# Routing in groups of four chunks, loads moved to SyncE, and transfers cut to 8 or 10 DMA engines, in a kernel of linear attention and experts on one core

## The chip, the cores and the metric

The kernel runs on one core of one Trainium2 chip. The metric is the device time of one execution in microseconds; lower is better. All times below are device microseconds.

## The reference

The first half is a linear attention with a 40 x 40 state per head, for 4 batches, 8 heads and 768 steps. The second half sends each of the resulting 3072 rows of 320 numbers to at most one of 8 experts.

```python
for t in range(S):                       # attention, S = 768, D = 40
    y[:, :, t] = np.einsum('bhd,bhde->bhe', rt, state)
    Sa = np.einsum('bhde,bhe->bhd', state, at)
    state_decay = state * wt[:, :, None, :] - np.einsum('bhd,bhe->bhde', Sa, bt)
    state = state_decay + np.einsum('bhd,bhe->bhde', vt, kt)
...
do_compute = x @ w_skip > 0              # experts, x is [3072, 320]
logits = xc @ w_gate; e_idx = np.argmax(logits, axis=1)
gate_w = probs[np.arange(len(xc)), e_idx]
h = np.maximum(xc[mask] @ w1[e], 0.0)    # w1 [8, 320, 1024], w2 [8, 1024, 320]
y[mask] = gate_w[mask, None] * (h @ w2[e])
out[do_compute] = xc + y
```

## The kernel before

**Attention.** The 768 steps are cut into 24 chunks of 32 steps. Two chunks are a pair h (12 of them), which is what `w`, `a`, `k`, `b` and `r` are loaded by. The loop `for c in range(NC)` in `attn` emits, for each chunk, a recurrence through the state: `ux` and `uq` (small matmuls, then ScalarE copies into the tile `R1t`, then a multiplication with a mask by GpSimd), `sst` (the new state), `rs`, and `yy`, which writes the 128 finished rows of the chunk into a tile `XS` and stores them from SyncE. Around it work for later chunks is spread: VectorE inverts the triangular factors (`tinv`, tiles `px` and `M`) and scans the decays, TensorE transposes and multiplies (`kbt`, `m1`, `m2`), GpSimd scales `k`, `b` and `a`.

**Routing.** `Moe.route` (from line 902 on) takes finished chunks: `xpose` transposes a chunk, `score` multiplies it with the 9 columns of skip and gate weights, `pick` finds the expert, and the rest ranks the rows within their expert, by a product of the one-hot rows `oh` with the triangle `s.tri` and with ones `s.one`. It adds a running `base` and scatters each chunk to a table `xg` by an indirect DMA from GpSimd. Before, one routing serves two chunks: eleven of them (started at c = 2, 4, ..., 22) and two of a single chunk at the end. Each `score` issues 12 matmuls per chunk, with 32 output rows each; the ranks take 8 matmuls per routing.

**Loads.** SyncE issues nearly all transfers, in the order of its queue. The function `load_rv` (line 357) loads `v` in the layout for the products with `r`, into `vvt`, `rrt` or `SCR`; `load_rr` (line 362) loads `r` into `rrt`; both take the issuing engine as an argument, which is GpSimd (`E=G`) from chunk 1 on. `cutl` loads rows 0 to 39 and 64 to 103 in two DMAs of 40 rows. `load_v` loads `v` a second time, as 16 pieces of 160 bytes in each of 32 rows, into `R1t`. `l1z` loads zeros, `idl` are constant blocks, `pad` fills the table `xg`, `load` (line 944) brings an expert's weights: of experts 0 and 1 at c = 20 and 22, of the others in the last part.

**The order.** Everything from the start up to chunk 21 is recorded by `Rec` and put in order by a planner (`Rec.plan`), a list schedule with costs of each instruction: `cost`, the transfer time of a DMA (`pipe`), a queue of DMA (`dq`), and a limit on how fast TensorE may go through blocks of 256 instructions, which take at least `BLK` us each (the constant `SLOW` stands beside it and is not used):

```python
pos+=t.k
while pos>=256*(blk+1):
    x=max(fin[i],ent+s.BLK); fin[i]=x; ent=x; blk+=1
```

The planner also may put a ScalarE copy out of PSUM on VectorE. Its order fixes the order on TensorE, ScalarE, VectorE, GpSimd and SyncE. A profile gives all recorded instructions the line of the call at the planner's end, L272, and those issued directly from chunk 22 on L134, which is the line of the recorder's call.

**Experts.** From about 490 us on the 8 experts are computed one after the other, in three products of rounded and remainder parts; the rows of each are scattered to the output by GpSimd.

Of the kernel before, what the change touches and what calls it, by code (L numbers as in the profile page):

```python
# [8 lines left out]
F32 = mybir.dt.float32  # L9
# [53 lines left out]
class Rec:  # L63
# [36 lines left out]
    def cost(s,e,op,w,r,a):  # L100
        sz=lambda x: int(np.prod([d[1] for d in list(x.ap)[1:]])) if len(list(x.ap))>1 else 1
        n=max(sz(x) for x in (w[:1]+r[:1]))
        if 'dma' in op: return (1.06,2.6) if 'ind' in op else (0.63 if e=='S' else 0.55,2.2)
# [12 lines left out]
        if op=='tensor_tensor_scan': return 0.02+0.00217*n,0  # L116
        if op=='transpose': return 0.08+0.00115*n*(1 if n<1000 else 1.6),0
        if op=='memset': return 0.04+0.0003*n,0
        if op=='reciprocal': return 0.17,0
        if op=='tensor_tensor': return (0.1 if ps and 'PSUM' not in str(w[0].space).upper() and n>199 else 0.06)+0.00105*n*(1 if ps or n<99 else 1.75),0  # L120
        return 0.12+0.00105*n,0
    def pipe(s,w,r):

        n=int(np.prod([d[1] for d in w.ap])); run=n
        for x in (w,r):
            q=1
            for st,k in reversed(list(x.ap)[0 if 'DRAM' in str(x.space).upper() else 1:]):
                if k>1 and st!=q: break
                q*=k
            run=min(run,q)  # L130
        p=w if 'DRAM' not in str(w.space).upper() else r
        return 4*n/min(6e5,5e3*max(16,p.ap[0][1]))+n/run*s.DSC/16
    def call(s,e,op,fn,a,k):
# [50 lines left out]
    def plan(s,keep=None):  # L184
# [33 lines left out]
        while done<N:  # L218
# [37 lines left out]
        s.st,s.fin,s.bank_of,s.en,s.span=st,fin,bank,en,max(fin)  # L256
    LET=0.7; FAR=1.0; ALT=1.0; FILL=None
    def keys(s):
# [46 lines left out]
def attn(ctx,tc,i,m,out,X):  # L305
# [50 lines left out]
    rvt={}  # L356
    def load_rv(c,E=G):
        if c>=NC: return
        t=VV[0] if c%2==0 else RR[1] if c==1 else VV[1]
        rvt[c]=t.rearrange("p (u t) -> p u t",u=16); cutl(E,rvt[c],i['vv'][c],c<4,128)  # L360
    rrt={}
    def load_rr(h,E=G):

        if h>=NH: return
        rrt[h]=RR[h%2].rearrange("p (u t) -> p u t",u=16); cutl(E,rrt[h],i['rr'][h],h<2,128)
    def load_v(c,x):
        if c>=NC: return
        SP.dma_start(R1[x][c%NR1][ao[x]:ao[x]+32,:,0:40],i['vt'][c,x])
    def scan_z(h,dst=None,E=None,rv=rv):
# [35 lines left out]
    def l1z(h,x):  # L405
        if h>=NH: return
        SP.dma_start(L1[x][h%NL][ao[x]:ao[x]+32].rearrange('p u c t -> p (u c t)'),i['zer'][0:32,0:1024])
    def l1a(h,x,E=None):
# [189 lines left out]
    def yy(c,x):  # L598
        if c<0: return
        if x==0: Yt[c]=ps_y.tile([128,8,40],F32,tag="py",name="psY")  # L600
        Y=Yt[c]
        R=R1[x][c%NR1]; l2=L2[x][(c//2)%NL2]; cc=c%2
        for hh in range(4):
            for b in range(4):
                u=4*b+hh
                TE.matmul(Y[32*b:32*b+32,2*hh+x,:],R[:,u,RW[cc]-32:RW[cc]],l2[:,cc,u,:],start=True,stop=True)
        if x==1:
            if cc==0: XS[c//2]=m.xp.tile([128,2,XW],F32,tag="XS",name="XS")
            xs=XS[c//2][:,cc,0:320]
            V.tensor_tensor(xs.rearrange("p (h e) -> p h e",h=8),Y,H[c//2]['WT',cc].rearrange("p h x e -> p (h x) e"),ALU.mult)  # L610
            SP.dma_start(ov[c],xs)
# [7 lines left out]
    if 1:  # L619

        with tc.manual_schedule(engines={ET.Pool}):
# [17 lines left out]
            for x in range(2): load_v(0,x)  # L639
            load_rv(0,SP); load_rr(0,SP); load_kb(2)  # L640
            scan_z(0,None,V); scan_d(0); scan_w(0,V); load_w(2)
# [8 lines left out]
            for x in range(2): l1a(1,x,V)  # L650
            load_a(2,L1t[:,3072:4096].rearrange("p (u t) -> p u t",u=16)); load_rv(1,SP)
            for b in range(4): kbt(0,b)
# [6 lines left out]
            for x in range(2):  # L659
                for c in range(2): SP.dma_start(L2[x][0][64*x:64*x+64,c],i['idl'][x,64*x:64*x+64])  # L660
            load_kb(3); load_w(3,alt[:,0:1041]); load_a(3,a1)
# [28 lines left out]
            for x in range(2):  # L690
                for c in range(2): SP.dma_start(L2[x][1][64*x:64*x+64,c],i['idl'][x,64*x:64*x+64])
        tg=iter(()); tn=[0]
# [154 lines left out]
class Moe:  # L847
# [46 lines left out]
    def route(s,XS,n,c0,last=None):  # L894
# [11 lines left out]
        yield  # L906
        rk=s.ps.tile([128,2*n,8],F32,tag="pp",name="rk")
# [233 lines left out]
```

## Time and profile before

| what | us |
|---|---|
| median of 3 runs | 624.01 (620.74 to 625.52) |
| the profiled execution | 625.9 |
| its span, first to last instruction | 624.0 |
| TensorE busy / VectorE busy | 470.0 / 472.7 |
| ScalarE busy / GpSimd busy | 390.0 / 315.5 |

The busy times are unions over the span. An engine can be idle in one stage and full in another, so the rows below are by stage. PE is TensorE's matmuls, PEld its weight loads, DVE VectorE, ACT ScalarE, POOL GpSimd, SPq SyncE's queue. `issue` is time in which an engine waited for nothing that the profile shows. A tile's name stands without its buffer number; the PSUM tiles are `pc`, `pq`, `ps`, `py`, `px`.

### The profile page before, as it was taken

Reading aid. Unit: us, or ns where it says so; the run is one execution under the profiler, and the core shown is the slowest. Engines: PE = TensorE matmul, PEld = TensorE weight load, DVE = VectorE, ACT = ScalarE, POOL = GpSimd, SP = SyncE. Lnnn points to the kernel's source line nnn. Section 1 sums busy time; section 2 is a strip of 40 time slices with the busy share of each in tenths; the row PEclk is TensorE's granted clock in tenths of the full one; section 3 lists DMA queues with packets and bytes.
Section 4 is the critical chain, followed back from the end, with each engine's and each line's share of the span. In section 5 each row is a group of like instructions: output and inputs, shape, how many; then the busy total and the mean of one; then the engine's idle time right before and its main releaser. Section 6 shows DMA issues by size and latency. Waiting matters only on the chain. (4 is left out here: it accounts for less than half of the span.)

```text
span 624.0 us, 28751 instructions
## 1 busy us (share of the span) xinstructions
PE 470.0 (75%) x12424; PEld 407.5 (65%) x12424; DVE 472.7 (76%) x1269; ACT 390.0 (62%) x982; POOL 315.5 (51%) x285
## 2 busy tenths in 40 slices
PE   0154327877787887887887789878977999999992
PEld 0143216666666666776776677667765799999992
DVE  6525894789997987998989879865783558898860
ACT  7073216878695877887696769577865455555510
POOL 4133626437491868477583853234223266666751
PEclk9997757899897998998798989989988999999997
DMA  8997232433452453425351534453663477775100
GB/s 190 251 270 226 78 99 65 130 81 92 93 137 75 108 143 100 133 67 147 87 153 40 144 98 109 101 153 95 167 168 93 123 220 232 240 225 156 43 18 18
DMA packets 64360, 80.59 MB, mean 129 GB/s; under 512 B 33698, under 2 KB 52719, under 8 KB 63124
## 3 DMA queue, kind: packets, MB, share of 16 engines
q1 hardware_dynamic: 58323, 64.55, 38.6%
q0 software_dynamic: 5904, 14.15, 8.2%
q8 instruction: 99, 1.62, 1.2%
q14 instruction: 34, 0.27, 0.1%
HBM read 67.80 MB, written 13.15 MB: 130 GB/s over the span
## 5 line engine op out<-in xcount | busy, mean ns | idle before, releaser
L272 ACT COPY R1t<-pc 32x288 f32<-32x288 f32 (+4 forms) x254 | 98.8, 389 | 38.1 <-PE pc L272 32.4
L272 POOL TENSOR_TENSOR R1t<-R1t,mc 64x512 f32<-64x512 f32 x43 | 55.5, 1292 | 70.9 <-ACT R1t L272 64.7
L272 DVE TENSOR_TENSOR px<-px,M 128x168 f32<-128x168 f32 (+10 forms) x240 | 61.2, 265 | 2.3
L134 POOL TENSOR_TENSOR WL<-WR,WH 128x1280 fp32r<-128x1280 f32 (+1 forms) x21 | 57.8, 2794 | 8.6 <-ACT WH L134 8.6
L272 POOL TENSOR_TENSOR WR<-WR,M 104x1024 f32<-104x1024 f32 x19 | 41.6, 2207 | 35.5 <-DVE M L272 22.9
L272 DVE TENSOR_TENSOR M<-M,px 128x168 f32<-128x168 f32 (+10 forms) x240 | 54.4, 255 | 2.0 <-DVE px L272 0.2
L272 DVE TENSOR_TENSOR_SCAN M<-M 104x1041 f32<-104x1041 f32 (+1 forms) x20 | 47.0, 2348 | 0.2
L272 ACT COPY R1t<-pq 32x256 f32<-32x256 f32 (+4 forms) x101 | 36.2, 358 | 8.4 <-PE pq L272 5.3
L134 ACT CAST WH<-WR 128x1024 fp32r<-128x1024 f32 (+1 forms) x35 | 39.6, 1132 | 0.0
L272 POOL DMA_INDIRECT xg<-XS,ix x20 | 24.1, 1206 | 29.9 <-DMA xg<-XS,ix 11.7
L134 POOL DMA_INDIRECT out<-ro,ti x16 | 15.8, 989 | 44.3 <-DVE ro L134 10.7
L272 PE MATMUL pc<-UX,TB 32*32 32x104 f32 (+1 forms) x1024 | 30.2, 245 | 9.0 <-issue 7.9
L134 ACT ACTIVATE hH<-pc 128x512 fp32r<-128x512 f32 x21 | 12.6, 599 | 37.8 <-PE pc L134 37.8
L134 DVE CAST ti<-xe 128x2 int32<-128x2 f32 x8 | 35.0, 4376 | 0.2
L272 PE MATMUL py<-L2t,R1t 128*32 128x40 f32 x1344 | 23.4, 208 | 12.1 <-issue 9.4
L134 PE MATMUL pc<-xH,WH 128*128 128x256 f32 x126 | 32.5, 283 | 0.0
L272 DVE TENSOR_TENSOR R1t<-pc,D 40x512 f32<-40x512 f32 (+1 forms) x44 | 26.6, 605 | 6.3 <-PE pc L272 4.2
L134 DVE TENSOR_TENSOR WL<-WR,WH 128x1024 fp32r<-128x1024 f32 (+1 forms) x19 | 23.8, 1253 | 9.9 <-ACT WH L134 9.4
L272 ACT COPY R1t<-ps 40x288 f32<-40x288 f32 (+4 forms) x72 | 27.5, 383 | 5.4 <-PE ps L272 4.2
L272 PE MATMUL ps<-R1t,L2t 128*40 128x72 f32 (+1 forms) x672 | 28.6, 233 | 2.8 <-ACT R1t L272 1.6
L272 PEld LDWEIGHTS pc<-UX,TB 32*32 32x32 f32 x1024 | 21.5, 107 | 14.0 <-issue 10.1
L272 PEld LDWEIGHTS py<-L2t,R1t 128*32 128x32 f32 x1344 | 17.7, 114 | 16.3 <-issue 11.7
(353 smaller groups left out, 1537.0 us busy)
## 6 DMA issues: line engine op xcount, KB each, us to landing
WR<-w SPq DMA_DIRECT2D x16, 640.0 KB
WR<-w SPq DMA_DIRECT2D x16, 512.0 KB
WR<-kb SPq DMA_DIRECT2D x16, 320.0 KB
WR<-w SPq DMA_DIRECT2D x16, 256.0 KB
R1t<-vt SPq DMA_DIRECT2D x48, 80.0 KB
out<-XS SPq DMA_DIRECT2D x24, 160.0 KB
rrt<-rr POOLq DMA_DIRECT2D x20, 160.0 KB, 5.4
vvt<-vv POOLq DMA_DIRECT2D x20, 160.0 KB, 6.1
```

The costliest lines, as they stand in the source:

```text
L134: if not s.on: return fn(*a,**k)
L272: for fn,a,k,own in s.tasks[i].calls: (fn if s.en[i]==s.tasks[i].e else s.nc.vector.tensor_copy)(*[at(x,own) for x in a],**{n:at(x,own) fo ...
```

## The change

1. One routing serves four chunks: `XS` holds four, routings start at c = 4, 8, 12, 16 and 20, one of two chunks at c = 22, and two of one chunk at the end as before. Twice as many steps of a routing are emitted per point.
2. `score` uses one matmul per third of the 320 columns with all 128 rows as output (3 per chunk, before 12). The ranks of a routing of n chunks take 1 + n matmuls with 128 output rows, which add up in PSUM what the running base of each further chunk was; VectorE adds the base once for all chunks and once for the next base. One memset is new.
3. `load_rv` and `load_rr` are issued from SyncE for every chunk.
4. The DRAM side of several DMAs is regrouped with an outer dimension of 8 (`load_v`, `l1z`, the `idl` blocks, `pad`, the weights of experts 0 and 1), which lays them on 8 DMA engines; weights of later experts have an outer dimension of 16. The DMAs of 40 rows are on 10 engines.
5. The planner's costs are others (`BLK` 3.4, `SLOW` 0, a DMA costs by 200 GB/s or 2 ns a piece, `FAR` 1.25), so the whole recorded order is another.
6. The scratch memory for GpSimd's DMA descriptors is 4096.

```diff
-    EX=...; BLK=3.6; SLOW=0.8; BW=2.7e5; DSC=0.012; AHEAD=2.5
+    EX=...; BLK=3.4; SLOW=0.0; BW=2.0e5; AHEAD=2.5; LAND=1.7
-        return 4*n/min(6e5,5e3*max(16,p.ap[0][1]))+n/run*s.DSC/16
+        return max(4*n/s.BW,n/run*0.002)
-                    x=max(fin[i],ent+s.BLK); fin[i]=x; ent=x; blk+=1
+                    x=max(fin[i],ent+s.BLK+s.SLOW*min(8.0,max(0.0,dq-ent))); fin[i]=x; ent=x; blk+=1
-            if t.x: dq=max(dq,fin[i]+1.0)+t.x; lat=max(lat+t.x,dq+1.2-fin[i])
+            if t.x:
+                a=fin[i]+(0.5 if e=='S' else 1.5); b=max(dq,a); dq=b+t.x
+                if t.x<0.3: b=a+0.4*(b-a)
+                lat=b+t.x+s.LAND-fin[i]
-    def load_rv(c,E=G):
+    def load_rv(c,E=SP):
-    def load_rr(h,E=G):
+    def load_rr(h,E=SP):
-        SP.dma_start(R1[x][c%NR1][ao[x]:ao[x]+32,:,0:40],i['vt'][c,x])
+        SP.dma_start(R1[x][c%NR1][ao[x]:ao[x]+32,:,0:40],i['vt'][c,x].rearrange('(a b) u d -> a b u d',a=8))
-            if cc==0: XS[c//2]=m.xp.tile([128,2,XW],F32,tag="XS",name="XS")
+            if c%4==0: XS[c//4]=m.xp.tile([128,4,XW],F32,tag="XS",name="XS")
-            if c%2==0 and c>0 and p==ROUTE[0]: rg=m.route(XS[c//2-1],2,c-2)
+            if c%4==0 and c>0 and p==ROUTE[0]: rg=m.route(XS[c//4-1],4,c-4)
+            if c==22 and p==ROUTE[0]: rg=m.route(XS[5][:,0:2],2,20)
...
                 next(rg,None)
+                if c<22: next(rg,None)
...
-            for q in range(4): nc.tensor.matmul(lg[32*q:32*q+32],xT[:b-a,k,32*q:32*q+32],s.wg[:b-a,k,:],start=k==0,stop=k==2)
+            nc.tensor.matmul(lg,xT[:b-a,k,:],s.wg[:b-a,k,:],start=k==0,stop=k==2)
...
-        for q in range(4): nc.tensor.matmul(rk[32*q:32*q+32,0:n,:],s.tri[:,32*q:32*q+32],oh,start=True,stop=True)
-        for q in range(4): nc.tensor.matmul(rk[32*q:32*q+32,n:2*n,:],s.one[:,0:32],oh,start=True,stop=True)
+        nc.tensor.matmul(rk,s.tri,s.oh[:,0:n+1],start=True,stop=False)
+        for j in range(n): nc.tensor.matmul(rk[:,j+1:n+1],s.one,oh[:,j].unsqueeze(1).broadcast_to([128,n-j,8]),start=False,stop=j==n-1)
         ps=wk.tile([128,n,8],F32,tag="pos",name="pos")
-        for j in range(n):
-            nb=wk.tile([128,8],F32,tag="base",name="base",bufs=3)
-            V.tensor_tensor(ps[:,j],rk[:,j],s.base,ALU.add)
-            V.tensor_tensor(nb,rk[:,n+j],s.base,ALU.add); s.base=nb
+        V.tensor_tensor(ps,rk[:,0:n],s.base.unsqueeze(1).broadcast_to([128,n,8]),ALU.add)
+        nb=wk.tile([128,8],F32,tag="base",name="base",bufs=3)
+        V.tensor_tensor(nb,rk[:,n],s.base,ALU.add); s.base=nb
...
+        n=8 if e<2 else 16
-        for k in range(2): SP.dma_start(r[:,1024*k:1024*k+1024],s.i['w1'][e,128*k:128*k+128])
+        for k in range(2): SP.dma_start(r[:,1024*k:1024*k+1024],s.i['w1'][e,128*k:128*k+128].rearrange('(a b) f -> a b f',a=n))
...
-    nc = bacc.Bacc("TRN2", target_bir_lowering=False, num_devices=1)
+    nc = bacc.Bacc("TRN2", target_bir_lowering=False, num_devices=1, dynamic_dma_scratch_size=4096)
```

## Rows read from the trace of the kernel before

**Rows 1.** Stages: us; PE, PEld, DVE, ACT, POOL busy; clock, DMA share, GB/s

```profile
0.00:90.00 90.00, 23.95 (x744) 20.34 (x747) 57.41 (x86) 36.83 (x91) 32.16 (x38) 0.84 0.68 181
90.00:130.00 40.00, 30.39 (x1184) 25.66 (x1178) 26.70 (x77) 26.86 (x72) 18.43 (x18) 0.81 0.39 103
130.00:410.00 280.00, 228.58 (x7674) 189.37 (x7672) 247.31 (x843) 214.04 (x591) 168.79 (x173) 0.94 0.43 109
410.00:475.00 65.00, 51.16 (x1704) 42.63 (x1692) 42.38 (x119) 47.91 (x135) 20.06 (x19) 0.95 0.51 140
...
490.00:624.00 134.00, 121.80 (x934) 121.06 (x934) 91.42 (x107) 60.32 (x81) 73.63 (x37) 0.97 0.49 147
```

**Rows 2.** Waits of PE from 90 to 475 us: us, times, longest

```profile
PE pc L272 <- issue: 12.1, 13, 3.8
...
PE py L272 <- issue: 9.4, 8, 3.2
PE ps L272 <- issue: 4.9, 5, 2.8
PE pq L272 <- issue: 4.2, 7, 1.4
...
PE py L272 <- POOL R1t L272: 2.5, 2, 2.2
```

**Rows 3.** Timeline of PE around 412 us: start, us, instruction, idle before

```profile
411.52 0.44 PE L272 MATMUL py<-L2t,R1t 128*32 128x40 f32 x25
415.14 0.24 PE L272 MATMUL py<-L2t,R1t 128*32 128x40 f32 x4 [3.17 <-issue]
```

**Rows 4.** The 4 us ahead of that stall, columns as in rows 1

```profile
408.00:412.00 4.00, 3.79 (x161) 3.10 (x156) 3.67 (x22) 3.79 (x11) 2.16 (x3) 1.00 0.93 267
```

**Rows 5.** SyncE's DMA queue, whole span: packets, MB, share of 16 engines

```profile
q1 hardware_dynamic: 58323, 64.55, 38.6%
```

**Rows 6.** The queue of instructions from 90 to 475 us, columns as in rows 5

```profile
q8 instruction: 83, 1.36, 1.6%
```

**Rows 7.** Waits of PE from 130 to 410 us for nothing shown

```profile
PE pc L272 <- issue: 9.1, 10, 3.8
PE py L272 <- issue: 6.2, 7, 1.6
...
PE pq L272 <- issue: 2.8, 6, 0.8
...
PE ps L272 <- issue: 1.8, 3, 1.2
```

**Rows 8.** Routing on DVE: busy us, mean ns of one | idle before

```profile
L272 DVE TENSOR_TENSOR pos<-pos,oh 128x16 f32<-128x16 f32 x10 | 5.1, 509 | 0.0
...
L272 DVE TENSOR_SCALAR ix<-sl 128x2 int32<-128x2 f32 x10 | 4.1, 406 | 0.0
...
L272 DVE TENSOR_TENSOR eq<-sc,mx 128x16 f32<-128x16 f32 x10 | 1.7, 169 | 0.1
```

**Rows 9.** A chunk's transposes and scores on PE: busy us, mean ns | idle before

```profile
L272 PE MATMUL ps<-mc,XS 128*128 128x128 f32 (+1 forms) x42 | 7.9, 298 | 1.3 <-ACT WT L272 1.1 <-ACT R1t L272 0.2
...
L272 PE MATMUL ps<-wg,xT 128*32 128x9 f32 (+1 forms) x216 | 4.5, 184 | 0.6 <-ACT xT L272 0.6
```

**Rows 10.** Loads and scatters that POOL issues, and its masking of R1t

```profile
L272 POOL TENSOR_TENSOR R1t<-R1t,mc 64x512 f32<-64x512 f32 x43 | 55.5, 1292 | 70.9 <-ACT R1t L272 64.7 <-DMA M<-M 4.5 <-issue 0.6
...
L272 POOL DMA_INDIRECT xg<-XS,ix x20 | 24.1, 1206 | 29.9 <-DMA xg<-XS,ix 11.7 <-DVE px L272 7.8 <-PE pc L134 4.9
...
L272 POOL DMA_DIRECT2D SCR<-vv x21 | 11.5, 551 | 20.6 <-PE pc L272 9.1 <-DVE TB L272 6.3 <-PE pq L272 4.6
L272 POOL DMA_DIRECT2D vvt<-vv x20 | 11.0, 557 | 7.2 <-PE pc L272 6.2 <-PE pq L272 1.0
L272 POOL DMA_DIRECT2D rrt<-rr x20 | 10.5, 532 | 14.7 <-PE pc L272 14.7
```

**Rows 11.** SyncE's issues of one tile: ns min/median/max

```profile
L272 SPq DMA_DIRECT2D R1t<-vt x46: 559/592/1188, 14.8 to 440.3; - x46
```

More of the change, by code (lines that the diff above doesn't have):

```diff
@@ L102, in cost @@
         n=max(sz(x) for x in (w[:1]+r[:1]))
-        if 'dma' in op: return (1.06,2.6) if 'ind' in op else (0.63 if e=='S' else 0.55,2.2)
+        if 'dma' in op: return (1.06,2.6) if 'ind' in op else (0.63 if e=='S' else 0.55,0.0)
         ps=any('PSUM' in str(x.space).upper() for x in r)
@@ L130, in pipe @@
             run=min(run,q)
-        p=w if 'DRAM' not in str(w.space).upper() else r
-        return 4*n/min(6e5,5e3*max(16,p.ap[0][1]))+n/run*s.DSC/16
+        return max(4*n/s.BW,n/run*0.002)
     def call(s,e,op,fn,a,k):
@@ L256, in plan @@
         s.st,s.fin,s.bank_of,s.en,s.span=st,fin,bank,en,max(fin)
-    LET=0.7; FAR=1.0; ALT=1.0; FILL=None
+    LET=0.7; FAR=1.25; ALT=1.0; FILL=None
     def keys(s):
@@ L406, in l1z @@
         if h>=NH: return
-        SP.dma_start(L1[x][h%NL][ao[x]:ao[x]+32].rearrange('p u c t -> p (u c t)'),i['zer'][0:32,0:1024])
+        SP.dma_start(L1[x][h%NL][ao[x]:ao[x]+32].rearrange('p u c t -> p (u c t)'),i['zer'][0:32,0:1024].rearrange('(a b) f -> a b f',a=8))
     def l1a(h,x,E=None):
@@ L639, in attn @@
             for x in range(2): load_v(0,x)
-            load_rv(0,SP); load_rr(0,SP); load_kb(2)
+            load_rv(0); load_rr(0); load_kb(2)
             scan_z(0,None,V); scan_d(0); scan_w(0,V); load_w(2)
@@ L650, in attn @@
             for x in range(2): l1a(1,x,V)
-            load_a(2,L1t[:,3072:4096].rearrange("p (u t) -> p u t",u=16)); load_rv(1,SP)
+            load_a(2,L1t[:,3072:4096].rearrange("p (u t) -> p u t",u=16)); load_rv(1)
             for b in range(4): kbt(0,b)
@@ L659, in attn @@
             for x in range(2):
-                for c in range(2): SP.dma_start(L2[x][0][64*x:64*x+64,c],i['idl'][x,64*x:64*x+64])
+                for c in range(2): SP.dma_start(L2[x][0][64*x:64*x+64,c],i['idl'][x,64*x:64*x+64].rearrange('(a b) u d -> a b u d',a=8))
             load_kb(3); load_w(3,alt[:,0:1041]); load_a(3,a1)
@@ L690, in attn @@
             for x in range(2):
-                for c in range(2): SP.dma_start(L2[x][1][64*x:64*x+64,c],i['idl'][x,64*x:64*x+64])
+                for c in range(2): SP.dma_start(L2[x][1][64*x:64*x+64,c],i['idl'][x,64*x:64*x+64].rearrange('(a b) u d -> a b u d',a=8))
         tg=iter(()); tn=[0]
@@ L702, in RP @@
                 next(rg,None)
+                if c<22: next(rg,None)
         def last22():
-            xl=XS[NC//2-1]
+            xl=XS[5][:,2:4]
             def onehot(q): V.tensor_scalar(m.P[q],m.io,m.sl[:,0:1],None,ALU.is_equal)
@@ L801, in attn @@
             T()
-            load_rv(c+2,G if c else SP)
-            if c%2 or c==0: load_rr((c+3)//2,G if c else SP)
+            load_rv(c+2)
+            if c%2 or c==0: load_rr((c+3)//2)
             if c<2: m.pad(2*c); m.pad(2*c+1)
@@ L860, in pad @@
     def pad(s,k):
-        s.nc.sync.dma_start(s.xg.rearrange("(q p) d -> p q d",p=128)[:,4*k:4*k+4],s.i['xpad'].unsqueeze(1).broadcast_to([128,4,XW]))
+        s.nc.sync.dma_start(s.xg.rearrange("(q p) d -> p q d",p=128)[:,4*k:4*k+4],s.i['xpad'].rearrange('(a b) d -> a b d',a=8).unsqueeze(2).broadcast_to([8,16,4,XW]))
     def xpose(s,X):
@@ L886, in pick @@
         m2=wk.tile([128,n],F32,tag="m2",name="m2"); V.reduce_max(m2,eq,axis=AX.X)
-        oh=wk.tile([128,n,8],F32,tag="oh",name="oh"); V.tensor_tensor(oh,eq,b3(m2),ALU.is_equal)
+        oh=wk.tile([128,5,8],F32,tag="oh",name="oh"); V.memset(oh[:,n],0.0); s.oh=oh; oh=oh[:,0:n]; V.tensor_tensor(oh,eq,b3(m2),ALU.is_equal)
         V.scalar_tensor_tensor(oh,pr[:,:,8:9].broadcast_to([128,n,8]),0.0,oh,ALU.is_gt,ALU.mult)
@@ L946, in load @@
         SP=s.nc.sync; r=s.raw[e%2]
-        for k in range(2): SP.dma_start(r[:,1024*k:1024*k+1024],s.i['w1'][e,128*k:128*k+128])
-        for k in range(2): SP.dma_start(r[64*k:64*k+64,2048:3072],s.i['w1'][e,256:320])
-        for k in range(2): SP.dma_start(r[:,3072+1280*k:4352+1280*k].rearrange("p (k d) -> p k d",k=4),s.i['w2'][e,512*k:512*k+512].rearrange("(k p) d -> p k d",p=128))
+        n=8 if e<2 else 16
+        for k in range(2): SP.dma_start(r[:,1024*k:1024*k+1024],s.i['w1'][e,128*k:128*k+128].rearrange('(a b) f -> a b f',a=n))
+        for k in range(2): SP.dma_start(r[64*k:64*k+64,2048:3072],s.i['w1'][e,256:320].rearrange('(a b) f -> a b f',a=n))
+        for k in range(2): SP.dma_start(r[:,3072+1280*k:4352+1280*k].rearrange("p (k d) -> p k d",k=4),s.i['w2'][e,512*k:512*k+512].rearrange("(k a b) d -> a b k d",k=4,a=n))
     def base_last(s):
```

6 lines of the change are left out of this document (3 added, 3 removed).

## Prediction

> **What bounds the kernel now.** I read the stages first. There are three. Until 90 us the loads and the first inverse run: the DMA engines are busy by 0.68 in the mean, and PE hardly works [rows 1]. From 490 us on PE is busy 121.8 of 134.0 us with the experts [rows 1]; the change leaves its instructions as they are, so I expect nothing there. Between them lie the 24 chunks, and that is where every edit works. In the long middle of it, 130 to 410 us, DVE is busy 247.3 of 280 us (88%), PE 228.6 (82%), ACT 214.0 (76%), POOL 168.8 (60%) [rows 1]. In the two ends, 90 to 130 and 410 to 475 us, DVE has room (26.7 of 40 and 42.4 of 65) and PE is the fullest [rows 1].
>
> Next the waits of PE. Its largest entries aren't a wait for another engine, but `issue`, for which the profile shows nothing: 12.1 + 9.4 + 4.9 + 4.2 = 30.6 us from 90 to 475 us [rows 2]. Of these 9.1 + 6.2 + 2.8 + 1.8 = 19.9 us lie in the middle [rows 7], so 10.7 us in the two ends. The timeline shows what they look like: at 411.96 us PE stops inside a group, after 25 of 32 products into the same `py`, for 3.17 us, and goes on with the very same group [rows 3]. A semaphore would stand between groups; an engine that stops inside one has no instructions. Instructions come by a DMA queue of their own: 83 packets in these 385 us, 1.36 MB / 83 = 16.4 KB each [rows 6], one per 4.6 us. Just before that stall the DMA engines were 0.93 busy with data [rows 4]. So I read the 30.6 us as instruction blocks that came late behind data.
>
> **The change part by part.** The sum is made against the profiled execution, 625.9 us, which is 1.9 us above the median of 624.0; I take the same 1.9 us off at the end.
>
> *Routing on DVE.* A routing has 18 DVE instructions: 15 of about 0.165 us (the comparison `eq` takes 169 ns), and three whose mean is larger, `oh` with 0.26, `pos` with 509 and `ix` with 406 ns [rows 8]: 15 x 0.165 + 0.26 + 0.51 + 0.41 = 3.65 us. A routing of four chunks has 17: two additions and two bases become one of each, one memset is new. The trace doesn't show these on 32 numbers a row instead of 16. From below they cost what they do now, from above eight of them double: + 8 x 0.169 = 1.35 us. I take 3.6 us, near the lower end, since the nearest row is the same instruction on half the numbers. Eleven routings become six, 5 x 3.6 = 18 us less DVE work (bounds 11 and 18). Eight of the eleven lie in the middle, where four replace them: 4 x 3.6 = 14.4 us off 247.3.
>
> *Scores and ranks on PE.* A chunk's score is 24 matmul records now, 4.5 us / 216 = 0.021 us each because small ones overlap, so 0.5 us per chunk [rows 9]. After it is 6 records with 128 output rows. From below they cost as the small ones, 0.13 us; from above as the transposes of 128 rows, 7.9 / 42 = 0.19 us each [rows 9], 1.1 us. That is -0.4 to +0.6 us per chunk; I take +0.15, because these move only 9 columns where the transposes move 128. Ranks go from 16 records for two chunks to 10 large ones for four: by the same two prices -0.5 to +1.2 us per four chunks; I take +0.6. In the middle, 16 chunks: 16 x 0.15 + 4 x 0.6 = 4.8 us more PE work (bounds -8 and +14). In return PE has fewer instructions: 18 records per chunk and, for ranks, 208 - 64 over the whole, 576 matmuls and as many weight loads, 1152 instructions. The three stages hold 21,104 matmuls and weight loads [rows 1] for 83 packets [rows 6], 254 a packet, so that is 4.5 packets fewer.
>
> *Transfers on 8 or 10 engines, loads to SyncE.* The 61 loads of `v` and `r` that POOL issues go to SyncE, and the broad transfers of SyncE are laid on 8 of the 16 engines. If the engine that brings PE's instructions is among those left free, the stalls go. Bounds: 0 and 30.6 us. Some stay, since blocks must still be fetched in turn; I take three quarters, 8.0 us in the two ends and 15 us in the middle. In the ends PE is the fullest engine and I count all 8.0 us. In the middle PE is relieved by 15 - 4.8 = 10 us and DVE by 14.4 us; ACT and the recurrence aren't, and each engine's waits are partly for the others. I count 8 us, a little over half of the two.
>
> *POOL* loses 61 issues of about 0.55 us, 33 us, and the waits before them, 20.6 + 7.2 + 14.7 us [rows 10]. It isn't full. What counts is the mask of `R1t` behind them in its queue, for which PE waited 2.5 us [rows 2]: I count 1 us (bounds 0 and 2.5). Four scatters of 1.2 us now come in a row, and before a scatter POOL already waited 11.7 us for the one before [rows 10]; the new order can place masks between them, so I count 0, at worst 2 us for each of five routings.
>
> *What is paid.* Per engine SyncE's queue moves 64.55 MB / (0.386 x 16 x 624 us) = 16.7 GB/s [rows 5]: 268 GB/s on 16 engines, 167 on 10, 134 on 8. A `vt` load of 80 KB goes from 0.3 to 0.6 us by that, hidden as long as it is issued a chunk ahead. A weight piece of 640 KB goes from 2.4 to 4.8 us; SyncE has two chunks for those of experts 0 and 1, so 0 (at worst 2.4 us for the last). In the start four `vt` and four constant blocks, 960 KB, need 7.2 instead of 3.6 us of 8 engines: between 0 and +3.6, I take +1, as PE and DVE there wait for other loads too. The smaller descriptor memory costs nothing that a row shows.
>
> Sum: -8.0 - 8 - 1 + 1 = -16 us: 609.9 by the profiled execution, **608 us** for the median.
>
> A rule speaks against this part. The Trainium skill, "DMA: Bandwidth & Descriptors", section "Rules for kernel authors", says to put a dimension that is a multiple of 16 outermost, because a smaller one confines the whole DMA to that many engines. By it the edit doubles transfer times and gives nothing; what it would do here is the second rival below, with the added cost of the fourth.
>
> **The rivals.**
> 1. *Both reliefs reach the end in full.* All stalls go (30.6 us) and POOL's 2.5 us, DVE being relieved enough not to take over: 624 - 33 = 591 us. For it: `issue` is the largest wait of PE. Against it: DVE at 88% and PE's waits on copies of `R1t` by ACT remain.
> 2. *The stalls stay.* They are the fetch's own pace, or the engine that fetches is one of those which now carry more. Then the 8 us of the ends and half of the middle are lost: 624 - 8 = 616 us. For it: no row tells which engine brings the instructions. Against it: the stall right behind 4 us of full DMA engines [rows 3, 4].
> 3. *The pace is the recurrence.* PE and DVE get room, and it turns into waits for copies of ACT and masks of POOL (70.9 us idle before them [rows 10]): 622 us, within 1%.
> 4. *SyncE's queue becomes the bound, and the kernel slower.* SyncE issues in order, at 0.59 us for a `vt` load [rows 11]. It takes over 61 issues, 36 us, and the waits for a free buffer before the `v` loads, 20.6 + 7.2 = 27.8 us [rows 10], and behind them stand the `vt` loads and the transposed blocks that the next chunk needs. Of 64 us a quarter (16 us) reaching PE eats the gain, a third and more makes it slower by over 1%: with 24 us, 632 us. For it: the queue is one, and its engines are now 8 or 10. Against it: no row of PE's waits names a `vt` load now, and the planner knows the queue.
>
> On the second: the Trainium skill, "Runtime: NRT & Kernel Launch", section "Instruction fetch mechanics", says that instructions are refilled in 16 KiB blocks and the cost of crossing a block is mostly hidden. The trace agrees on the block (16.4 KB) and not on the cost (30.6 us); if the rule held, the stalls would be something else and rival 2 decides.
>
> **How the numbers follow.** Forecast 608 us (own range 600 to 614): 0.50. Rivals 1 to 4: 0.16, 0.14, 0.11, 0.09. A measurement of this kernel can tell about 1%, 6 us, from no change. Faster by over 1% (below 617.8): the forecast, rival 1, and 0.10 of rival 2's 0.14, which lies near the bound: 0.76. Within 1%: 0.04 + 0.11 = 0.15. Slower: 0.09. The range reaches to rival 1 and over rival 3, and leaves out rival 4 and what lies below rival 1: 590 to 624 us.
>
> **What would show it.** Right: PE's `issue` waits between 90 us and the experts' start fall from 30.6 to below 10 us; some 4 or 5 packets less in the instruction queue of that stage; five routings of 32 numbers a row on DVE and its busy time in the chunks down by about 18 us; no load issued by POOL; the experts still take about 134 us. Wrong: `issue` stays at 20 us or more (rival 2); PE waits for `DMA R1t<-vt` or ACT and POOL waits grow by what `issue` loses (rivals 4 and 3); scores that cost PE over 1 us a chunk.

## The result and the profile after

601.84 us in the median of 4 runs (599.05 to 606.82), against 624.21 us (620.74 to 625.52, 4 runs): a ratio of 0.9659 [0.958, 0.9738], faster by 3.4%. The forecast was 608 us in a range of 590 to 624. Executions of one kernel lie up to 3.6% apart here (one of the experiments gave 601.5 us at a mean granted clock of 0.952 and 623.2 at 0.925), so kernels are compared by ratios, and a profile is read for where its time lies. The profiled execution of after took 606.82 us with a span of 605.1.

The stages of the changed kernel answer to [rows 1], with the same columns:

```profile
0.00:90.00 90.00, 37.27 (x1228) 32.07 (x1230) 72.77 (x106) 46.03 (x117) 40.83 (x44) 0.77 0.73 195
90.00:130.00 40.00, 34.22 (x1214) 29.23 (x1214) 34.08 (x115) 30.92 (x83) 23.78 (x16) 0.87 0.39 111
130.00:390.00 260.00, 225.86 (x6928) 190.02 (x6923) 219.50 (x714) 207.71 (x573) 139.29 (x114) 0.95 0.42 115
390.00:455.00 65.00, 52.79 (x1393) 45.21 (x1393) 37.77 (x90) 39.87 (x113) 13.32 (x12) 0.84 0.44 125
...
471.00:605.00 134.00, 124.45 (x939) 122.71 (x938) 90.80 (x110) 60.38 (x81) 73.34 (x37) 0.98 0.49 147
```

The experts again take 134 us. The surprise is the first row: by 90 us DVE has worked 72.77 us instead of 57.41. Two marks cut the span better than round times: the first copy of `TB` out of `M`, when the first inverse is done, and the last product into `XS`, when the last chunk's output is. The views of these two tiles (count, duration, first and last start) in the kernel before:

```profile
L272 DVE COPY TB<-M x2: 568/600/632, 89.1 to 90.6; 128x512 f32<-128x512 f32 x2
...
L134 DVE TENSOR_TENSOR XS<-py,WT x3: 491/492/493, 461.9 to 480.2; 128x320 f32<-128x320 f32 x3
```

and in the changed one:

```profile
L274 DVE COPY TB<-M x2: 549/574/600, 70.0 to 71.4; 128x512 f32<-128x512 f32 x2
...
L133 DVE TENSOR_TENSOR XS<-py,WT x3: 491/492/492, 439.8 to 462.2; 128x320 f32<-128x320 f32 x3
```

The start is 89.1 - 70.0 = 19.1 us shorter; the chunks take 480.2 - 89.1 = 391.1 and 462.2 - 70.0 = 392.2 us. **In these two profiles all of the gain lies in the start, which the prediction made 1 us longer, and none in the chunks, where it put 16 us.** The mean granted clock of TensorE in the chunks was 0.92 of full speed before and 0.90 after (the two windows further down), so a few us of gain there may be hidden by it.

Why the start is shorter shows in the timelines of DVE and PE. DVE before:

```profile
22.40 0.25 DVE L272 COPY XS<-mc 128x2 f32<-128x2 f32 x2 [10.68 <-DMA mc<-mc]
...
22.63 2.33 DVE L272 TENSOR_TENSOR_SCAN L2t<-L2t,M 104x1041 f32<-104x1041 f32 x1
...
46.49 0.32 DVE L272 STREAM_TRANSPOSE M<-pc 128x128 f32<-128x128 f32 x1 [10.99 <-ACT M L272]
```

DVE after:

```profile
11.96 2.33 DVE L274 TENSOR_TENSOR_SCAN L2t<-L2t,M 104x1041 f32<-104x1041 f32 x1
...
30.43 0.32 DVE L274 STREAM_TRANSPOSE M<-pq 128x128 f32<-128x128 f32 x1 [1.38 <-ACT M L274]
...
44.28 2.06 DVE L274 COPY XS<-mc 128x4 f32<-128x4 f32 x1
```

The routing's copy of token numbers (`XS<-mc`), which nobody needs for 100 us, stood at the head of DVE's queue and waited 10.68 us for the constants, with the scan into `L2t` (the second half's) behind it. The new order has the copy at 44.28 us, that scan at 11.96 instead of 22.63, and the first transposes 16 us earlier.

But the copy is not the wait that ended last. DVE had caught up by 35.5 us (46.49 - 10.99) and then waited again, through copies of ACT, for PE. PE's queue before, and then after:

```profile
30.26 1.12 PE L272 MATMUL pc<-rrt,vvt 128*64 128x64 f32 x16 [6.83 <-DMA rrt<-rr]
...
39.66 1.07 PE L272 MATMUL pq<-rrt,rrt 128*64 128x32 f32 x16 [6.54 <-DMA rrt<-vv]
...
41.52 0.96 PE L272 MATMUL pc<-mc,WR 104*128 104x104 f32 x4
```

```profile
26.18 1.59 PE L274 MATMUL pc<-mc,WR 104*128 104x104 f32 x8
...
39.95 0.69 PE L274 MATMUL pc<-rrt,vvt 128*64 128x64 f32 x16
```

The transposes of `WR` (`mc,WR`) lead to the first inverse. Before, two groups of products of `r` and `v` stood ahead of them and waited 6.83 and 6.54 us for their loads; the new order has the transposes first and those products behind.

In the chunks the waits of PE changed as forecast, and its work too. The waits from 90 to 455 us answer to [rows 2]:

```profile
PE py L133 <- POOL R1t L274: 7.1, 1, 7.1
PE pq L274 <- issue: 5.2, 5, 1.7
PE py L274 <- POOL R1t L274: 4.8, 2, 3.8
...
PE pc L274 <- issue: 3.0, 8, 1.0
...
PE py L274 <- issue: 2.4, 4, 1.0
```

`issue` fell from 30.6 to 5.2 + 3.0 + 2.4 = 10.6 us; the wait for POOL's mask of `R1t` rose from 2.5 to 11.9. That the `issue` stalls are waits for instructions, as the prediction read them, shows in the traces when each stall is laid beside the packets of the instruction queue: before, 28 of 37 stalls from 90 to 475 us (28.9 of 32.3 us, two small entries more than the 30.6) end 1.1 to 1.9 us after such a packet has landed, and after, 13 of 17 (9.0 of 10.6 us). Between the two marks, the windows of before and then of after:

```profile
89.00:480.00 391.00, 315.97 (x10763) 261.45 (x10760) 319.17 (x1048) 291.50 (x806) 208.01 (x209) 0.92 0.44 114
```

```profile
70.00:462.00 392.00, 333.41 (x10241) 280.23 (x10241) 304.50 (x950) 290.12 (x800) 185.09 (x150) 0.90 0.43 120
```

In these bounds PE's `issue` goes from 32.4 to 14.1 us, 18.3 less, and its busy time from 315.97 to 333.41, 17.4 more. The groups of scores (`wg,xT`) and ranks (`oh,mc`) on PE say where that comes from (busy us, mean ns); after:

```profile
L274 PE MATMUL ps<-wg,xT 128*128 128x9 f32 (+1 forms) x84 | 13.5, 269 | 0.2 <-ACT SS L274 0.2
...
L274 PE MATMUL ps<-oh,mc 128*128 128x40 f32 (+4 forms) x30 | 4.9, 311 | 0.9 <-DVE oh L274 0.9
L133 PE MATMUL pq<-wg,xT 128*128 128x9 f32 (+1 forms) x24 | 4.4, 292 | 1.2 <-ACT R1t L133 1.2
L274 PE MATMUL pc<-wg,xT 128*128 128x9 f32 (+1 forms) x24 | 3.9, 269 | 0.0
...
L133 PE MATMUL pq<-oh,mc 128*128 128x16 f32 (+2 forms) x14 | 2.6, 311 | 0.0
L274 PE MATMUL pc<-oh,mc 128*128 128x40 f32 (+4 forms) x20 | 2.6, 271 | 0.8 <-ACT R1t L274 0.8
...
L274 PE MATMUL pq<-wg,xT 128*128 128x9 f32 (+1 forms) x12 | 1.9, 263 | 0.0
```

Scores: 13.5 + 4.4 + 3.9 + 1.9 = 23.7 us for 144 records, 0.165 us each and 0.99 us a chunk, where 576 records at the 0.021 us of [rows 9] made 12.1. Ranks: 4.9 + 2.6 + 2.6 = 10.1 us, where before these four groups make 4.3:

```profile
L272 PE MATMUL ps<-oh,mc 128*32 128x16 f32 x80 | 1.7, 193 | 2.2 <-DVE R1t L272 1.7 <-DVE oh L272 0.5
L134 PE MATMUL pq<-oh,mc 128*32 128x8 f32 (+1 forms) x48 | 1.0, 190 | 0.8 <-DVE oh L134 0.5 <-DVE sm L134 0.4
L272 PE MATMUL pc<-oh,mc 128*32 128x16 f32 x48 | 0.9, 186 | 0.2
L272 PE MATMUL pq<-oh,mc 128*32 128x16 f32 x32 | 0.7, 204 | 0.0
```

Together 11.6 + 5.8 = 17.4 us, as much as PE's busy time grew. What the stalls gave, the longer matmuls took. The Trainium skill, "TensorEngine Tiling (Array Packing)", "Key Properties", says that tiles of the array load weights and multiply in parallel. The trace bears that out: a 32-row record lasts 0.18 us [rows 9] and costs 0.021, while a 128-row one costs 0.165.

The last chunks are where a lead was lost again. POOL's timeline there:

```profile
412.18 1.01 POOL L274 DMA_INDIRECT xg<-XS,ix  x1 [0.40 <-DMA xg<-XS,ix]
416.86 0.98 POOL L274 DMA_INDIRECT xg<-XS,ix  x1 [3.68 <-DMA xg<-XS,ix]
424.08 1.34 POOL L274 DMA_INDIRECT xg<-XS,ix  x1 [6.24 <-DMA xg<-XS,ix]
426.92 1.26 POOL L274 TENSOR_TENSOR R1t<-R1t,mc 64x512 f32<-64x512 f32 x1 [1.50 <-DMA xg<-XS,ix]
```

Each scatter waits for the one before it to land, and behind the last stands the mask for which PE waited the 7.1 us. Over the span, the scatters' group answers to [rows 10]:

```profile
L274 POOL DMA_INDIRECT xg<-XS,ix x20 | 26.4, 1319 | 52.6 <-DMA xg<-XS,ix 32.6 <-PE ps L274 10.8 <-DVE M L274 3.6
```

32.6 us of waiting for the previous scatter, 11.7 before.

### The profile page after: what moved, and what is told of

Its sections match the earlier page's. It is cut to its first block, busy times and chain, and to the rows that moved or that the text cites. A ratio compares the mean times of both kernels' runs of the same rounds, so it can differ in the third digit from the quotient of the medians.

```text
span 605.1 us, 27499 instructions
## 1 busy us (share of the span) xinstructions
PE 489.1 (81%) x11848; PEld 428.5 (71%) x11848; DVE 462.3 (76%) x1173; ACT 389.6 (64%) x979; POOL 293.1 (48%) x224
## 5 line engine op out<-in xcount | busy, mean ns | idle before, releaser
L274 ACT COPY R1t<-pc 32x288 f32<-32x288 f32 (+4 forms) x253 | 96.8, 383 | 18.5 <-PE pc L274 13.1
L274 POOL DMA_INDIRECT xg<-XS,ix x20 | 26.4, 1319 | 52.6 <-DMA xg<-XS,ix 32.6
L274 ACT COPY R1t<-pq 32x416 f32<-32x416 f32 (+4 forms) x105 | 41.4, 395 | 9.6 <-PE pq L274 7.4
L133 ACT ACTIVATE hH<-pc 128x512 fp32r<-128x512 f32 x21 | 12.6, 598 | 40.5 <-PE pc L133 40.5
L133 DVE CAST ti<-xe 128x2 int32<-128x2 f32 x8 | 33.2, 4148 | 0.2
L133 PE MATMUL pc<-xH,WH 128*128 128x256 f32 x126 | 32.4, 283 | 0.1
L274 PE MATMUL pc<-UX,TB 32*32 32x72 f32 (+1 forms) x960 | 26.9, 248 | 4.4 <-ACT UX L274 3.0
L274 PE MATMUL py<-L2t,R1t 128*32 128x40 f32 x1344 | 23.2, 211 | 7.7 <-POOL R1t L274 4.8
L133 PE MATMUL ps<-WH,hH 128*128 128x320 f32 x88 | 27.5, 313 | 0.0
L133 PE MATMUL ps<-WL,hH 128*128 128x320 f32 x88 | 27.1, 308 | 0.0
L133 PE MATMUL ps<-WH,hL 128*128 128x320 f32 x88 | 27.1, 308 | 0.0
L133 PE MATMUL pc<-xH,WL 128*128 128x256 f32 x126 | 27.0, 280 | 0.0
L274 ACT COPY R1t<-ps 40x288 f32<-40x288 f32 (+3 forms) x63 | 22.8, 363 | 5.7 <-PE ps L274 4.6
```

What stands on the lines that cost most here:

```text
L133: if not s.on: return fn(*a,**k)
L274: for fn,a,k,own in s.tasks[i].calls: (fn if s.en[i]==s.tasks[i].e else s.nc.vector.tensor_copy)(*[at(x,own) for x in a],**{n:at(x,own) fo ...
```

## The experiments

They ran in three batches, each beside its own runs of the kernel before (medians of 615.5, 621.2 and 619.8 us). The row `after` is the result above, with its own runs of before. The table has the median and the profiled execution, and what that profile shows: the mean granted clock in the chunks as a share of full speed, when the first inverse is done, the stretch from there to the last chunk's output, and in it PE's busy time and its `issue` (windows cut to whole microseconds).

| kernel | ratio to before | median | profiled | clock | first inverse | chunks | PE busy | issue |
|---|---|---|---|---|---|---|---|---|
| before | 1 | 624.2 | 625.9 | 0.92 | 89.1 | 391.1 | 316.0 | 32.4 |
| after | 0.966 [0.958, 0.974] | 601.8 | 606.8 | 0.90 | 70.0 | 392.2 | 333.4 | 14.1 |
| e1_planner_only | 0.988 [0.983, 0.993] | 608.1 | 608.1 | 0.91 | 66.5 | 395.1 | 315.8 | 39.7 |
| e2_old_planner | 1.034 [1.023, 1.046] | 635.5 | 643.5 | 0.88 | 88.8 | 406.8 | 338.6 | 16.0 |
| e3_16_engines | 0.980 [0.972, 0.988] | 602.0 | 614.7 | 0.89 | 65.9 | 399.5 | 334.6 | 16.7 |
| e4_route_two | 0.979 [0.970, 0.987] | 601.2 | 603.3 | 0.90 | 66.5 | 392.7 | 333.5 | 21.3 |
| after_again | 0.975 [0.969, 0.981] | 605.0 | 605.0 | 0.90 | 68.1 | 394.5 | 333.5 | 15.9 |
| e5_pool_loads | 0.994 [0.990, 0.998] | 617.8 | 621.4 | 0.92 | 85.2 | 390.7 | 324.7 | 23.2 |
| e8_late_two | 0.968 [0.961, 0.976] | 598.5 | 588.4 | 0.95 | 65.6 | 380.2 | 322.3 | 22.0 |
| e10_score32 | 0.964 [0.958, 0.970] | 599.9 | 607.7 | 0.90 | 67.7 | 397.6 | 323.7 | 30.6 |
| e11_late_token | 1.026 [1.019, 1.033] | 634.1 | 633.8 | 0.90 | 90.3 | 397.5 | 319.8 | 22.1 |
| e13_late_pairs | 0.973 [0.966, 0.980] | 603.1 | 610.2 | 0.88 | 69.2 | 398.3 | 342.8 | 20.8 |
| e14_late_pairs_score32 | 0.950 [0.943, 0.957] | 588.2 | 601.8 | 0.90 | 67.5 | 391.6 | 324.4 | 31.1 |
| e15_before_sync_loads | none given | 618.7 | 623.1 | 0.94 | 88.8 | 388.7 | 308.4 | 26.4 |

The chunk lengths go with the clock: 398.3 to 406.8 us at 0.88 and 0.89, 391.6 to 397.6 at 0.90 and 0.91, 390.7 and 391.1 at 0.92, 388.7 at 0.94 and 380.2 at 0.95. So does PE's busy time: 342.8 us in e13 at 0.88 and 322.3 in e8 at 0.95, for the same matmuls. A difference of some us in these two columns is therefore not put down to an edit unless the clocks agree.

**e1_planner_only**: the kernel before with the planner's new costs and nothing else.

```
- BLK=3.6; SLOW=0.8; BW=2.7e5; DSC=0.012
+ BLK=3.4; SLOW=0.0; BW=2.0e5; LAND=1.7
- return 4*n/min(6e5,5e3*max(16,p.ap[0][1]))+n/run*s.DSC/16
+ return max(4*n/s.BW,n/run*0.002)
...
```

> The kernel before with the new planner's costs alone (routing of two, loads from GpSimd, 16 engines as before). Theory P, the gain came at the start, from an order that no longer takes large transfers for landed before they are: the first inverse is done (first copy into TB) at 70 to 73 us instead of 89.1, and the time is 603 to 610 us. Theory F, it came from instruction blocks that no longer wait behind data: issue of PE in the chunks stays at 25 us or more, time 618 us or more. Theory R, it came from fewer routing instructions on VectorE: no gain, 620 us or more.

608.14 us beside 615.54. The first inverse comes at 66.5 us: the start is the planner's doing. The stalls stay (39.7 us). The start is 22.6 us shorter than in the profile of before, but the median only 7.4 us. That is about half of the 13.6 and 14.3 us that e3 and e4, which have the other edits too, gain in the same batch; what the other half comes from is not shown.

**e2_old_planner**: the changed kernel with the old costs, the same diff the other way.

> The changed kernel with the old planner's costs. Theory P: the start is long again, first copy into TB at 85 us or later, time 618 to 626 us. Theories F and R: their parts stay, so 602 to 610 us.

635.47 us, slower than before. The start is back (88.8 us; DVE waits 10.2 us for `mc` at its head again, PE 6.6 and 7.0 us for the loads of `rrt`), the stalls are not (16.0 us), and the chunks are the longest of all (406.8 us, in its longest execution, at a clock of 0.88). No theory had named this: in the changed kernel the old costs lose 33.5 us against e3, while the new ones gained 7.4 in the kernel before. The parts of the change don't add up.

**e3_16_engines**: the changed kernel with the old access patterns; the order of instructions stays the same on all five engines.

```
- SP.dma_start(R1[x][...],i['vt'][c,x].rearrange('(a b) u d -> a b u d',a=8))
+ SP.dma_start(R1[x][...],i['vt'][c,x])
...
```

> The changed kernel with the old access patterns, so vt, zeros, constant blocks, pads and the first two experts' weights lie on 16 engines again; the order on all five engines is the same as in the changed kernel. Theory F: PE's issue in the chunks goes from 10.6 us back to 20 to 30, time up by 8 to 16 us, 610 to 618. Theory P: issue may rise, but the time stays within 1%, 596 to 608. If the weights on 8 engines cause the loss in the last four chunks (from 392 to 456 us in the changed kernel, against 46.5 us for the same chunks before), that stretch gets 8 us or more shorter and the time falls.

601.98 us, and PE's stalls from 66 to 466 us are:

```profile
PE pc L274 <- issue: 7.5, 7, 3.2
...
PE pq L274 <- issue: 6.9, 6, 3.0
...
PE py L274 <- issue: 2.1, 2, 1.6
```

16.5 us in these, as in the changed kernel (14.1 and 15.9). Confining transfers to 8 or 10 engines is not what removed the stalls, nor does it cost anything that shows. The chunks of 399.5 us are those of its longest execution.

**e4_route_two**: routings of two chunks, the new matmuls kept.

```
- if c%4==0 and c>0 and p==ROUTE[0]: rg=m.route(XS[c//4-1],4,c-4)
+ if c%2==0 and c>0 and p==ROUTE[0]: rg=m.route(XS[(c-2)//4][:,(c-2)%4:(c-2)%4+2],2,c-2)
...
```

> The changed kernel with routings of two chunks again (with the new 128-row matmuls). Theory R: VectorE's busy time up by 14 to 18 us, time up by 5 to 9 us, 607 to 611. Theory P: time within 1%, 596 to 608, and the scatters in the last chunks no longer stand four in a row, so the masks wait less there.

601.22 us: the same time as e3 in its batch. The chunks take 392.7 us; at chunk 19 it is later than after (405.7 and 392.1 us), and from there to the last chunk it takes 53.5 us where after takes 70.1. The larger routing brings nothing that shows in the time.

**after_again**: the changed kernel as the control for the next three.

> The changed kernel once more, as the control for the three variants run beside it. Every theory: 600 to 604 us, the first inverse done at 66 to 70 us, 8 to 12 us of issue stalls on PE between 90 and 460 us, and some 60 us for the last four chunks.

605.04 us.

**e5_pool_loads**: the `v` and `r` loads on POOL again.

```
- def load_rv(c,E=SP):
+ def load_rv(c,E=G):
...
- def load_rr(h,E=SP):
+ def load_rr(h,E=G):
```

> The changed kernel with its v and r loads issued by POOL again. Theory A (the stalls went because these loads left the queue that POOL feeds): PE's issue stalls between 90 and 460 us come back to 25 to 30 us and the time is 4 to 10 us above the control. Rival (the stalls went because the 128-row matmuls are 5% fewer instructions, or with the new order): 8 to 15 us of stalls, and at most 2 us more, for 40 loads of 0.55 us on an engine that is not the bound.

617.83 us, 12.8 above the control, but not for the reason given. The stalls rose only to 23.2 us, and the chunks took 390.7 us, no longer than the control's 394.5. The loss is the start (85.2 us, 17.1 later than the control's): the first loads went to POOL as well, which the expectation had not counted, and DVE's queue begins so:

```profile
22.20 0.28 DVE L274 COPY R1t<-pq 32x128 f32<-32x128 f32 x1 [15.50 <-ACT R1t L274]
```

A copy ahead of the first scan waits 15.5 us, and PE waits 19.3 us for what DVE makes behind it.

**e8_late_two**: routings of four up to chunk 15, of two behind it.

```
- if c%4==0 and c>0 and p==ROUTE[0]: rg=m.route(XS[c//4-1],4,c-4)
+ if c%4==0 and 0<c<20 and p==ROUTE[0]: rg=m.route(XS[c//4-1],4,c-4)
+ if c in (18,20) and p==ROUTE[0]: rg=m.route(XS[4][:,c-18:c-16],2,c-2)
```

> The changed kernel with routings of four up to chunk 15 and of two behind it, so that no four scatters stand in a row near the end. Theory A (four scatters in a row hold up the block masks and lose the lead there): the lead at chunk 19 stays (390 to 394 us), the last four chunks take 46 to 52 us instead of 64, and the time is 8 to 14 us below the control. Rival (the lead at chunk 19 is work put off, which has to be done at the end whoever scatters): the last chunk ends within 3 us of the control's, and so does the time.

598.49 us. In this kernel the second half of a late pair can run ahead of its chunk's output and then routes older rows, so it computes something else; all 24 scatters are there, but a wait is missing. Its chunks took 380.2 us in a profile with a granted clock of 0.949, where the control had 0.914, so that length can't be laid beside the others. e13 repeats it with every step behind its output.

**e10_score32**: the scores by 32-row matmuls again.

```
- nc.tensor.matmul(lg,xT[:b-a,k,:],s.wg[:b-a,k,:],...)
+ for q in range(4): nc.tensor.matmul(lg[32*q:32*q+32],xT[:b-a,k,32*q:32*q+32],s.wg[:b-a,k,:],...)
```

> The changed kernel with the scores by twelve matmuls of 32 rows again, instead of three of 128. Theory A (a 128-row score matmul costs PE its 0.16 us, 0.5 us a chunk more than the twelve): PE is 8 to 11 us less busy, and the time 3 to 6 us below the control. Rival (each of the 864 instructions more brings instruction fetches nearer to the bound): 3 to 4 packets more on that queue, 3 to 8 us more of issue stalls, and a time 0 to 4 us above the control.

599.94 us, 5.1 below the control; the two intervals overlap. Theory A was right about PE's busy time (9.8 us less at the same clock) and the time, the rival about more stalls, and by more than it said (14.7 us). The score groups:

```profile
L274 PE MATMUL ps<-wg,xT 128*32 128x9 f32 (+1 forms) x264 | 5.6, 182 | 3.0 <-issue 1.8 <-ACT xT L274 1.3
L274 PE MATMUL pq<-wg,xT 128*32 128x9 f32 (+1 forms) x120 | 2.4, 182 | 0.0
L133 PE MATMUL pq<-wg,xT 128*32 128x9 f32 (+1 forms) x96 | 2.4, 202 | 1.2 <-ACT R1t L133 1.2
L274 PE MATMUL pc<-wg,xT 128*32 128x9 f32 (+1 forms) x96 | 2.2, 183 | 1.2 <-issue 0.8 <-ACT xT L274 0.4
```

12.6 us, 11.1 less than with 128 rows; and its waits between the marks:

```profile
PE pc L274 <- issue: 10.2, 11, 3.0
PE py L274 <- issue: 8.9, 6, 4.7
...
PE pq L274 <- issue: 5.9, 6, 1.7
PE ps L274 <- issue: 5.1, 7, 1.8
```

The stalls are back at 30.6 us. Work of PE and stalls change places here.

**e11_late_token**: the kernel before with the copy of token numbers tied to the chunk's output.

```
- V.tensor_copy(XS[:,:,321],s.tok[:,c0:c0+n])
  for j in range(n):
+     V.scalar_tensor_tensor(XS[:,j,321:322],XS[:,j,0:1],0.0,s.tok[:,c0+j:c0+j+1],ALU.mult,ALU.add)
      xT=s.xpose(XS[:,j])
```

> The kernel before with one edit: the token numbers are copied into a routing tile chunk by chunk, behind the chunk's own output (zero times its first column, plus the number), so that the copy can't be placed ahead of the second scan and wait there for the constants; 24 instructions of DVE in place of 12. Theory A (VectorE's 10.7 us for the constants at 11.7 us sets the length of the start): the second scan starts at 12 to 14 us, the first inverse is done at 77 to 81 us instead of 89, and the time is 7 to 11 us below the kernel before. Rival (the large transfers set the start, the copy only stood beside them): the first inverse is done at 86 to 90 us and the time is within 3 us.

634.1 us, slower than before: a miss for both in the time, but the start is the rival's. The second half's scan does start at 11.91 us, but the old costs put another instruction, which needs a product of PE, a little behind it, and PE's own queue is as before:

```profile
11.91 2.33 DVE L272 TENSOR_TENSOR_SCAN L2t<-L2t,M 104x1041 f32<-104x1041 f32 x1
...
32.34 0.49 DVE L272 COPY WT<-pc 128x320 f32<-128x320 f32 x1 [13.96 <-PE pc L272]
...
46.67 0.32 DVE L272 STREAM_TRANSPOSE M<-pc 128x128 f32<-128x128 f32 x1 [5.48 <-ACT M L272]
```

```profile
38.96 1.07 PE L272 MATMUL pq<-rrt,rrt 128*64 128x32 f32 x16 [6.66 <-DMA rrt<-vv]
```

So DVE's wait moved by one instruction, the first transposes came at 46.67 us (before 46.49), and the first inverse at 90.3 us. With the copy gone the start is as long as before: PE's wait for late loads holds it as well. Why the chunks became 6.4 us longer the run doesn't say; the edit made a new order everywhere.

**e13_late_pairs**: as e8, and `if c<18: next(rg,None)` instead of `if c<22`, so that the late pairs step as before.

> The changed kernel with routings of four up to chunk 15, and from chunk 16 on routings of two, each step at the place that it has in the kernel before. Theory A (four scatters in a row delay the block masks at the end): the last four chunks take 46 to 54 us instead of 60 to 64, and the time is 5 to 10 us below the changed kernel, ratio to the kernel before 0.955 to 0.965. Rival (the chunks are held by PE, whose matmuls and waits add up to the same 391 to 395 us in every version): first inverse to last output 390 to 396 us, and a ratio of 0.968 to 0.977.

603.05 us. From chunk 19's output to chunk 22's, the stretch that the expectation means, it took 50.7 us (410.7 to 461.4) where after took 63.9, as Theory A said. But chunk 19 came 18.6 us later than in after, and the ratio is the rival's: taking the four scatters apart at the end brings nothing by itself.

**e14_late_pairs_score32**: e10's and e13's edits together.

> The late pairs and the scores by twelve matmuls of 32 rows, together. If both count: ratio to the kernel before 0.950 to 0.960. Rival (PE's stalls for instructions take the place of the longer score matmuls, as 30.6 us of them did with the 32-row scores alone): PE about 10 us less busy and as many us more of issue stalls, and a ratio of 0.963 to 0.975.

588.21 us, at the lower end of "both count": the best kernel of the study, with an interval that doesn't touch after's in either batch. Its four shorter executions had granted clocks of 0.923 to 0.943, higher than most others, but the clock isn't all of it: at 0.923 it took 590.8 us, after_again 602.4 at 0.922 and e13 599.5 at 0.919. Yet between its marks it looks like the others:

```profile
67.00:459.00 392.00, 324.41 (x10658) 271.51 (x10658) 307.48 (x958) 292.25 (x812) 183.20 (x150) 0.90 0.44 120
```

PE is 9 us less busy than in after and has 31.1 us of stalls, as the rival said. This profile is of its longest execution (601.8 us), so it can't show where the gain lies. That stays open.

**e15_before_sync_loads**: the kernel before with the `v` and `r` loads on SyncE, e5's edit the other way in the chunks alone.

> The kernel before with its v and r loads issued by SyncE, nothing else. Theory A (loads in the queue that POOL feeds slow the fetching of instructions): issue stalls between 89 and 480 us fall from 32 to 20 to 24 us, as they rose from 16 to 23 where the changed kernel got these loads back on POOL. Rival (the fetches are slow for the number of instructions alone): 29 to 36 us. Of the time: if the stalls lie on the path, 6 to 10 us below the kernel before; if something else takes their place, within 4 us.

618.7 us in the median beside 619.82; no ratio is given, since its executions spread from 601.5 to 623.2 us. Stalls of 26.4 us: between the two expectations. Its start is that of before (88.8 us), and so is the time.

## Why the prediction was right, and where it was wrong

The time lay in the range and the sign was right, but that was luck: two errors in the sum cancelled. The prediction named the start and the chunks by +1 and -16 us; the profiles show -19.1 and +1.1.

*The start: +1 us, measured -19.1.* This is the step that failed. The prediction counted there only what the changed transfers would cost, and took the waits of PE and DVE "for other loads" as cover; those waits were what could be saved. It priced the planner's new costs nowhere, though the diff makes a large transfer dearer. In the four profiles with the old costs (before, e2, e11, e15) PE waits 13.2 to 13.6 us for the loads of `rrt` ahead of the transposes, DVE waits 10.2 to 14.0 us for one instruction that comes too early, and the first inverse is done at 88.8 to 90.3 us. In e5, where the first loads went to POOL, DVE waits 15.5 us and PE 19.3 for DVE, and it is done at 85.2. In the nine others PE begins with the transposes, the longest wait of DVE from 8 to 60 us is 1.4 us, and it is done at 65.6 to 70.0 us. e1 and e2 show that the costs decide it: the new ones alone give 66.5 us, the old ones under all the rest 88.8. The old estimate divided by as much as 600 GB/s, the new one by 200, and the queue moved about 268 [rows 5]; that this one constant among the new costs is the cause is likely, but no run changes it alone. What PE's wait and DVE's are worth singly is not shown either: e11 took one instruction of DVE away, and PE still held the transposes.

*Stalls: 30.6 to 7.6 us forecast, 10.6 measured; but not by that mechanism.* They are waits for instructions, as the prediction said, but freeing engines of data is not what ended them. e3 gives the transfers all 16 engines in the same order and keeps the relief. What goes with the stalls is the form of the scores, and with it the number of matmuls: with 128 rows the eight profiles after, after_again, e2, e3, e4, e5, e8 and e13 have 14.1 to 23.2 us; with 32 rows before, e1, e10, e11, e14 and e15 have 22.1 to 39.7. The loads' queue may add to it (e5 7 us more, e15 6 us less), less than the spread within a group. So the rule of the Trainium skill on confined transfers, "DMA: Bandwidth & Descriptors", "Rules for kernel authors", found no price here. Nor is a gain by the edit shown: the ratios are 0.980 with all engines, 0.966 and 0.975 without, but in three batches and with intervals that overlap. The signs that the prediction named for itself stood on the line: `issue` at 10.6 us where it wanted less than 10, and scores at 0.99 us a chunk where over 1 us was to tell against it.

*16 us less in the chunks: measured 1.1 us more, at a clock lower by 0.02.* The failed term is the price of scores and ranks: 0.15 us a chunk and 0.6 per four, 7.2 us for all 24, taken near the lower bound; they cost 17.4 us, near the upper bound of 24 x 0.6 + 6 x 1.2 = 21.6. The nearest row was the transposes, 0.19 us, as the prediction said itself; the 9 columns don't make a 128-row matmul cheap. PE's work and its stalls summed to 348.4 us before and 347.5 after, and to 349.4 and 354.3 in after_again and e10, which differ by the scores and the order that follows from them: relief from stalls was taken up by work. Over all fourteen profiles the sum runs from 334.8 us at a clock of 0.94 to 363.6 at 0.88, so it is no constant.

*DVE: 18 us less, measured 319.17 - 304.50 = 14.7 in the chunks.* Right in size, without effect on the end. On 32 numbers most of its instructions were near the lower bound (`oh` 183 to 185 ns, `ix` 156), but the comparison `eq`, the row from which the price was taken, doubled (169 to 342 ns).

*POOL: -1 us, and scatters in a row 0.* The 61 loads left, but PE's wait for masks rose by 9.4 us, and the waits between scatters by 20.9 us. In sum that is the worst case named, 2 us for each of five routings, but 7.1 us of it came at one place, behind the last of the scatters near 425 us. e4 and e13 show that removing it shortens nothing by itself.

*SyncE's queue* (rival 4): no wait of PE names a `vt` load. The rival that came nearest is the third, with no gain in the chunks; its 622 us failed by the start. Its mechanism held for POOL's masks alone: PE's largest wait for ACT's copies of `R1t` fell from 9.9 to 5.4 us, and what took the place of the stalls was PE's own work.

## What to carry to other kernels

Before pricing an edit to a planner's costs, list the waits of every engine in the first tenth of the span, with what stands behind the waiting instruction, and follow which of them ends last. An early instruction that waits for a late load holds all that stands behind it in its queue, and a changed transfer estimate moves it; but where two engines wait, as here, freeing one gives nothing (e11). When PE stalls for instructions, fewer and larger matmuls turn the stall into work unless each large one costs less than the records it replaces; add busy time and stalls, at the same clock, before counting either as a gain. And two edits that are worth nothing alone (e13) or little (e10) gave 2.5% together (588.21 us beside e13's 603.05), for a reason that stays open: in a planned kernel, where each edit makes a new order, a part's price was not the same in another order.

## What was not expected of the hardware

In the changed kernel a scatter issued behind another waited up to 6.47 us for it to land; four of them, with one mask between the first two, held POOL from 408 to 425 us. A 128-row matmul of 9 columns cost 0.165 us of PE, eight times the 0.021 us of a 32-row one, and four of the small ones half of it. Most stalls of PE for instructions end 1.1 to 1.9 us after a packet of instructions has landed (28 of 37 before). And with 12,424 matmuls instead of 11,848 the stalls differed by a factor of two between two orders of nearly the same work (22.1 us in e11, 39.7 in e1), without the chunks following: 397.5 and 395.1 us.
